# Fetching an expert's second weight matrix in eight gathers of 1 KB rows, and splitting the first in its own order

## The chip, the cores and the metric

The kernel runs on one core of a Trainium2 chip. The metric is device time in microseconds of that core. A core has a matrix engine (TensorE, PE in the profile, its weight loads PEld), VectorE (DVE), ScalarE (ACT), GpSimd (POOL) and SyncE (SP), each with a queue of its own that it works through in order, and 16 DMA engines that all of them feed.

## The reference

The input `x` is 8 sequences of 2496 tokens with 256 features. A Fourier filter along the sequence comes first, then a mixture of 8 experts with a strict capacity.

```python
X = np.fft.rfft(x, axis=1)
y = np.fft.irfft(X * (filt_r + 1j*filt_i)[None], n=x.shape[1], axis=1)   # 8 x 2496 x 256
x = y.reshape(19968, 256)
logits = x @ w_gate                       # 19968 x 8
for idx in np.argsort(-logits.flatten()): # greedy: best pair of token and expert first
    tok, e = idx // 8, idx % 8
    if assigned[tok] < 0 and counts[e] < 2496:
        assigned[tok] = e; counts[e] += 1
for e in range(8):
    h = np.maximum(x[assigned == e] @ w1[e], 0)   # 2496 x 256 by 256 x 1024
    out[assigned == e] = h @ w2[e]                # by 1024 x 256
```

All of it is float32. Every expert ends with exactly 2496 tokens, so its work has a fixed size; which expert is settled next is known only on the chip.

## The kernel before

**Stages.** `Fft` does the filter by matmuls (`s1`, `s2`, `tr`, `inv1`, `inv2`) and writes the filtered tokens to the DRAM buffer `xs` and the logits to `lg`. `Route` finds the assignment in eight phases; each settles one more expert by a search over thresholds (`counts`, `threshold`), and `places` turns it into row numbers: `xid`, where the tokens lie in `xs`, and `oid`, where they belong in `out`. `Ffn` does the experts. From about 526 us on, the product of one expert runs on TensorE while the phases that settle the next ones run in between.

**One expert** (`Ffn.run`) takes its 2496 tokens in five groups of up to 512. `gather` fetches a group's tokens from `xs` in four indirect DMAs of 128 rows of 1 KB each (L814, tile `xg`, 8 buffers). `turn` transposes them on TensorE (L828, tile `ptr`, two halves `h` per group) and splits them into a rounded high part and a low part, by a cast on ScalarE (L831, `xo`) and a subtraction on VectorE (L832, `z`). `first` multiplies by the first matrix, 128 hidden units at a time (f from 0 to 7), in three matmuls for each half of the features (high by high, high by low, low by high; L850, tile `pz`), applies the ReLU and splits the result into `hl` (L856 on ScalarE, L864 or L867 on VectorE, for some of them L860 on GpSimd). Then `run` multiplies by the second matrix (L899, tile `py`, two PSUM buffers), 128 tokens at a time, ScalarE copies the result to `y` (L909, four buffers), and an indirect DMA from GpSimd scatters it to `out` (L910). `pz` and `ptr` share four PSUM buffers. The transposes of the next group stand between the products of the current one: those of group g+1 come after f = 2 and f = 4 of group g.

**The weights.** `Ffn.weights` allocates `raw[0]` and `raw[1]` (tile `wr`, one buffer of 128 x 2048 for each matrix) and the split copies `hl` (two buffers each; the profile shows the first matrix's as `w0h` and `w0l`, the second's as `w1h` and `w1l`). `load(k)` issues an indirect gather from GpSimd (L793) with row numbers `widx` that `expert` computes on VectorE from the expert's number (L659). Each fetches 128 rows of 8 KB. For the first matrix (256 x 1024) partition q gets feature rows 2q and 2q+1. For the second (1024 x 256) partition q gets its rows 8q to 8q+7, so that block f of the products holds the hidden units 8q+f. The columns of the first matrix must then be taken in that order too, and the split of the first matrix reads every eighth column:

```python
src = src.rearrange("p (j q f) -> p j f q", j=2, f=8)[:, j, 4*h:4*h+4]
```

`split` works on a quarter of a matrix at a time: part 0 to 3 are the first matrix's, 4 to 7 the second's. Each is a cast on ScalarE (L807) and a subtraction on VectorE (L808) of 128 x 512.

**What sets the order.** TensorE's order is written out by hand: `Pump` feeds the phases of the routing between the products by lags and due times that stand in the code. The other engines' orders come from a planner that simulates the program with costs of its own and takes what is ready, in the order of the code; `issue_after` pins an instruction behind another on its engine. At the start of the expert stage the code issues the first matrix's gather behind a small copy on GpSimd (L999), then the four splits of the first matrix, the four token gathers of group 0, behind these the gather of the second matrix, the two transposes of group 0, the four splits of the second matrix, and then the run of the expert, whose first act is the token gathers of group 1. For every later expert both matrices are gathered as soon as its phase has found it (`on_w`), while the expert before is still at work, and the splits are dealt out one by one, one for every `PACE` = 5 steps of the products.

Of the kernel before, what the change touches and what calls it, by code (L numbers as in the profile page):

```python
# [8 lines left out]
BF, F16, I32 = mybir.dt.bfloat16, mybir.dt.float16, mybir.dt.int32  # L9
AF, OP, AX = mybir.ActivationFunctionType, mybir.AluOpType, mybir.AxisListType  # L10
# [34 lines left out]
def constants():  # L45
    f = np.float32
    n1, k = np.arange(N1), np.arange(K1)
    c, s = _cs(n1[:, None] * k[None], N1)
# [27 lines left out]
    E = flat(E).astype(f)  # L76
    Eh = _round(E)
    p = np.arange(128)
    row = np.zeros((128, 115))
    row[:, 0:8] = np.arange(8, 0, -1)  # L80
    row[:, 8:16] = np.arange(8)
    row[126, 16] = row[127, 17] = -1
    row[:, 25:32] = G * np.arange(1, 8)
    row[:, 32], row[:, 33], row[:, 34] = p, 64 * (p % 39) + p // 39, p // 39
    pw = np.zeros((128, 11, 7))
    ic = np.zeros((128, 84), np.int64)
# [374 lines left out]
class Route:  # L461
# [10 lines left out]
    def setup(s):  # L472
        nc, i = s.nc, s.i
        t = lambda n, sh, dt=F32: s.cp.tile(sh, dt, name=n)
        s.row = t("row", [128, 115])
        s.pw = t("pw", [128, 11, 7])
        s.ic = t("ic", [128, 84], I32)
        s.tri = t("tri", [117, 118], F16)
# [2 lines left out]
        nc.sync.dma_start(s.ic, i['cInt'])  # L481
        nc.gpsimd.dma_start(s.tri, i['cTri'])
        s.desc, s.eids = s.row[:, 0:8], s.row[:, 8:16]
        s.k22, s.pcol = s.row[:, 25:32], s.row[:, 32:33]
        s.mS = {nj: s.row[:, 40+16*k:56+16*k] for k, nj in enumerate((9, 3, 7))}
        s.mJ = {nj: s.row[:, 88+9*k:88+9*k+nj] for k, nj in enumerate((9, 3, 7))}
        s.ones16 = t("ones16", [128, 128], F16)
# [140 lines left out]
    def phase(s, ph):  # L628

        nc = s.nc  # L630
# [20 lines left out]
        s.want()  # L651
        vc, need, tot, mem = v("vc", [128, 1]), v("need", [128, 1]), v("tot", [117, 4]), v("m0", [117, S])
        tb, pf = v("tb", [117, 2], F16), v("pf", [117, 4])
        ev, ej, eid, widx = v("ev", [128, 8]), v("ej", [128, 8]), v("eid", [128, 1]), v("widx", [128, 1], I32)

        def expert():
            nc.vector.tensor_scalar(ev, s.val, vc, None, op0=OP.is_equal)
            nc.vector.scalar_tensor_tensor(ej, ev, 1.0, s.eids, op0=OP.mult, op1=OP.mult, accum_out=eid)
            nc.vector.scalar_tensor_tensor(widx, eid, 128.0, s.pcol, op0=OP.mult, op1=OP.add)  # L659
        if ph < 7:  # L660
            n = s.n
            T = s.T
# [112 lines left out]
class Ffn:  # L775


    def __init__(s, tc, i, xs, out, cp, ww, zp, ps):
        s.tc, s.nc, s.xs, s.out, s.ww, s.zp, s.ps = tc, tc.nc, xs, out, ww, zp, ps
        s.w1 = i['moe_w1'].rearrange("e (q k) f -> (e q) (k f)", k=2)  # L780
        s.w2 = i['moe_w2'].rearrange("e (q f) d -> (e q) (f d)", f=8)
        s.id = cp.tile([128, 128], F32, name="id")
        make_identity(s.nc, s.id)
        s.scat = []
        s.wt, s.xg, s.xT = {}, {}, {}

    def weights(s, e, widx):
        nc = s.nc
        raw = [s.ww.tile([128, 2048], F32, name=f"wr{k}", bufs=1) for k in range(2)]
        off = bass.IndirectOffsetOnAxis(ap=widx[:, :1], axis=0)  # L790
        hl = [[s.ww.tile([128, 2048], F32R, name=f"w{k}{h}", bufs=2) for h in 'hl'] for k in range(2)]
        s.wt[e] = (raw, hl)
        s.load = lambda k: nc.gpsimd.indirect_dma_start(out=raw[k], out_offset=None, in_=(s.w1, s.w2)[k], in_offset=off).ins  # L793

    def split(s, e, part):

        nc = s.nc
        raw, hl = s.wt[e]
        k, h = divmod(part, 4)
        src, (hi, lo) = raw[k], hl[k]  # L800
        if k == 0:
            h, j = divmod(h, 2)
            src = src.rearrange("p (j q f) -> p j f q", j=2, f=8)[:, j, 4*h:4*h+4]
            hi, lo = (t.rearrange("p (j f q) -> p j f q", j=2, f=8)[:, j, 4*h:4*h+4] for t in (hi, lo))
        else:
            src, hi, lo = (t[:, 512*h:512*h+512] for t in (src, hi, lo))
        nc.scalar.copy(hi, src)  # L807
        nc.vector.tensor_tensor(lo, src, hi.bitcast(F32), op=OP.subtract)  # L808

# [315 lines left out]
```

## Time and profile before

| | |
|---|---|
| runs shown | 1575.35, 1579.18, 1582.28 us (median 1579.18) |
| profiled execution | 1580.15 us, span 1578.4 us |
| granted TensorE clock | 0.958 of full speed, mean |
| TensorE busy | 1419.3 us (90%) |
| VectorE / ScalarE / GpSimd busy | 979.5 / 727.5 / 537.5 us |
| weight gathers (L793) | 16, 16.0 us of GpSimd |
| token gathers (L814) and scatters (L910) | 160 and 160, 171.4 and 173.7 us of GpSimd |
| splits of the first matrix (L808) on VectorE | 32, 36.4 us |
| splits of the second matrix (L808) on VectorE | 32, 21.5 us |

Times in a trace are microseconds from the span's start. A line of a timeline gives the start, the duration, the engine, the source line, the operation, the tile written, the tiles read, the shapes and a count of merged instructions; in brackets stands how long the engine was idle before it and what it then waited for. The waits of an engine are given as total, number and longest. A row of windows gives its length, the busy times of TensorE, its weight loads, VectorE, ScalarE and GpSimd with their numbers of instructions, then the granted clock, the DMA engines' share and GB/s.

### The profile page before, as it was taken

To read this page: it belongs to the slowest core of one execution; us is meant where nothing else is said; L and a number is where in the kernel's file an instruction comes from. 1 tells how busy PE (TensorE), PEld (TensorE's weight loads), DVE (VectorE), ACT (ScalarE), POOL (GpSimd) and SP (SyncE) were. 2 spreads that over 40 slices of the span, in tenths; PEclk is the share of its full clock that TensorE was granted. 3 is DMA by queue.
4 is the path that set the end of the run, shared out by engine and by line. 5 is a ranking of instruction groups with operands and counts; after the bars stand their busy time and mean duration, and the time that the engine had idled before them with its cause. 6 is when DMAs were issued, how large, how long until landed. Compare 5 with 4: busy or idle time off the path is not lost.

```text
span 1578.4 us, 27475 instructions
## 1 busy us (share of the span) xinstructions
PE 1419.3 (90%) x10374; PEld 1240.7 (79%) x10374; DVE 979.5 (62%) x2620; ACT 727.5 (46%) x1703; POOL 537.5 (34%) x557
## 2 busy tenths in 40 slices
PE   2788779799898689999999989999999999999998
PEld 1687658689664378888878878888879889899898
DVE  2677556588544856876776686786696772622322
ACT  4465445566444642643553453453462453632322
POOL 0233223335210242354264434343433443333311
PEclk9899989899979789999999999999999999999999
DMA  8878898845878510211121211211211221111100
GB/s 151 146 111 170 189 186 131 170 93 141 190 217 278 185 53 21 88 59 33 71 63 43 77 45 50 79 51 43 89 44 40 92 98 41 48 44 41 47 28 26
DMA packets 121096, 148.75 MB, mean 94 GB/s; under 512 B 70629, under 2 KB 93755, under 8 KB 118659
## 3 DMA queue, kind: packets, MB, share of 16 engines
q1 hardware_dynamic: 97994, 70.63, 22.6%
q0 software_dynamic: 17840, 60.34, 11.8%
q10 hardware_dynamic: 5129, 16.01, 2.9%
q8 instruction: 82, 1.34, 0.4%
q14 instruction: 51, 0.42, 0.1%
HBM read 84.47 MB, written 62.50 MB: 93 GB/s over the span
## 4 chain that ended last, share of the span: by engine, by line
PE 43%; DVE 10%; issue 7%; ACT 2%; POOL 1%; DMA 1%; another core or an unknown queue 0%; POOLq 0%; DVEq 0%; ACTq 0%
PE py L899 20%; PE pz L850 19%; PE rt L558 2%; PE ptr L828 2%; DVE hl L864 1%; POOL out L910 1%; ACT lg L718 1%; DVE hl L867 1%; DVE w0l L808 1%; DVE w1l L808 1%; DMA wr<-moe_w,widx 1%; DVE Gm L550 1%; DVE OH L749 1%; PE rt L755 1%; DVE tmp L639 0%
## 5 line engine op out<-in xcount | busy, mean ns | idle before, releaser
L899 PE MATMUL py<-w1h,hl 128*128 128x256 f32 x2496 | 485.6, 287 | 3.3 <-DVE hl L867 2.8
L899 PEld LDWEIGHTS py<-w1h,hl 128*128 128x128 f32 x2496 | 403.3, 192 | 7.5 <-DVE hl L867 3.7
L899 PE MATMUL py<-w1l,hl 128*128 128x256 f32 (+1 forms) x1280 | 360.1, 283 | 0.0
L910 POOL DMA_INDIRECT out<-y,oid x160 | 173.7, 1086 | 452.3 <-ACT y L909 410.5
L856 ACT ACTIVATE hl<-pz 128x512 fp32r<-128x512 f32 (+1 forms) x320 | 186.4, 587 | 218.1 <-PE pz L850 182.2
L850 PE MATMUL pz<-xo,w0h 128*128 128x512 f32 (+1 forms) x640 | 265.4, 415 | 12.3 <-DVE hl L864 6.7
L850 PE MATMUL pz<-xo,w0l 128*128 128x512 f32 (+1 forms) x640 | 250.1, 391 | 0.0
L850 PE MATMUL pz<-z,w0h 128*128 128x512 f32 (+1 forms) x640 | 249.3, 389 | 0.8 <-DVE z L832 0.8
L899 PEld LDWEIGHTS py<-w1l,hl 128*128 128x128 f32 (+1 forms) x1280 | 242.3, 189 | 2.0
L864 DVE SCALAR_TENSOR_TENSOR hl<-pz,hl 128x512 fp32r<-128x512 f32 x227 | 155.0, 687 | 121.0 <-ACT hl L856 119.5
L814 POOL DMA_INDIRECT xg<-xs,xid x160 | 171.4, 1071 | 134.3 <-issue 43.3
L909 ACT COPY y<-py 128x256 f32<-128x256 f32 x152 | 56.3, 371 | 294.5 <-PE py L899 254.5
L850 PEld LDWEIGHTS pz<-xo,w0h 128*128 128x128 f32 x640 | 122.7, 192 | 33.6 <-DVE hl L864 9.0
L207 PE MATMUL p<-cS,xr 117*128 117x120 f32 x688 | 102.2, 293 | 42.5 <-ACT xr L195 30.7
L850 PEld LDWEIGHTS pz<-xo,w0l 128*128 128x128 f32 x640 | 121.4, 190 | 24.1
L215 ACT COPY Y<-p 64x240 f32<-64x240 f32 (+1 forms) x304 | 116.0, 381 | 44.0 <-PE p L207 38.3
L850 PEld LDWEIGHTS pz<-z,w0h 128*128 128x128 f32 x640 | 122.3, 191 | 17.3 <-DVE z L832 1.8
L207 PEld LDWEIGHTS p<-cS,xr 117*128 117x128 f32 x688 | 94.0, 208 | 49.0 <-ACT xr L195 30.6
L230 POOL TENSOR_TENSOR P<-P 128x256 f32<-128x256 f32 x80 | 59.7, 746 | 209.6 <-DVE P L228 209.2
L550 DVE TENSOR_TENSOR Gm<-M,thr 117x1232 bf16<-117x1232 f32 (+2 forms) x80 | 104.4, 1316 | 0.2
L222 PE MATMUL p<-cW,Y 128*128 128x128 f32 x640 | 92.9, 280 | 1.3 <-DVE Q L229 1.2
L222 PEld LDWEIGHTS p<-cW,Y 128*128 128x128 f32 x640 | 82.9, 194 | 7.8 <-issue 3.7
(234 smaller groups left out, 2255.8 us busy)
## 6 DMA issues: line engine op xcount, KB each, us to landing
xt<-x SPq DMA_DIRECT2D x24, 838.5 KB
zd<-zt SPq DMA_DIRECT2D x140, 128.0 KB
z<-zd SPq DMA_DIRECT2D x26, 600.0 KB
xs<-xo SPq DMA_DIRECT2D x12, 585.0 KB
xs<-xo ACTq DMA_DIRECT2D x11, 585.0 KB
xs<-Y ACTq DMA_DIRECT2D x9, 585.0 KB
zd<-zt ACTq DMA_DIRECT2D x20, 128.0 KB
xg<-xs,xid POOLq DMA_INDIRECT x160
```

Of the source, the lines that this page charges most:

```text
L207: s.lastmm = nc.tensor.matmul(p[:, q-q0, :120], xv[:, q-24*h], s.cS1, start=True, stop=True).ins
L215: (nc.vector.tensor_copy if t in ((5,) if b else (1, 3, 5, 7, 9)) else nc.scalar.copy)(dst, src)
L222: nc.tensor.matmul(p[:, k], s.Y1[b][:, 4*g+k, dh*128:dh*128+128], s.cW[:, 4*g+k], start=True, stop=True)
L230: nc.gpsimd.tensor_tensor(P[:, :, :64], P[:, :, :64], P[:, :, 64:], op=OP.subtract)
L550: nc.vector.tensor_tensor(Gm[:, s0:s1, :m], s.M[:, s0:s1].unsqueeze(2).to_broadcast([117, s1 - s0, m]), thr[:117].unsqueeze(1).to_broadcas ...
L814: s.lastg = s.nc.gpsimd.indirect_dma_start(out=xg[:n], out_offset=None, in_=s.xs, in_offset=bass.IndirectOffsetOnAxis(ap=ids[0][:n, t:t+1] ...
L850: nc.tensor.matmul(p[:, :n], w[:, sl], x[:, k, :n], start=m == 0, stop=m == 5)
L856: s.lasta = nc.scalar.activation(h[:, :n], p[:, :n], AF.Relu).ins
L864: nc.vector.scalar_tensor_tensor(l[:, :n], p[:, :n], 0.0, h[:, :n].bitcast(F32), op0=OP.max, op1=OP.subtract)
L899: nc.tensor.matmul(p[:a.stop-a.start], hs[g][f][:, a], b[:, 256*f:256*f+256], start=m == 0, stop=m == 8 * len(terms) - 1, skip_group_check ...
L909: s.lasta = nc.scalar.copy(y, p).ins
L910: st = nc.gpsimd.indirect_dma_start(out=out_rows, out_offset=bass.IndirectOffsetOnAxis(ap=ids[1][:w, 4*g+t:4*g+t+1], axis=0), in_=y[:w], i ...
```

## The change

The second matrix is gathered in its own order: eight gathers of 128 rows of 1 KB, gather f fetching rows 128f to 128f+127 into columns 256f to 256f+255 of `raw[1]`. Block f of the products then holds the hidden units 128f to 128f+127, and the split of the first matrix reads 512 neighbouring columns. The order in which its four parts are taken stays: the first halves of both feature rows, then the second halves. `widx` grows from one column to nine, by a second operation on VectorE and eight columns more in the constant `row`.

```diff
-    row = np.zeros((128, 115))
+    row = np.zeros((128, 123))
...
+    row[:, 115:123] = p[:, None] + 128 * np.arange(8)
...
-            nc.vector.scalar_tensor_tensor(widx, eid, 128.0, s.pcol, op0=OP.mult, op1=OP.add)
+            nc.vector.scalar_tensor_tensor(widx[:, 0:1], eid, 128.0, s.pcol, op0=OP.mult, op1=OP.add)
+            nc.vector.scalar_tensor_tensor(widx[:, 1:9], eid.to_broadcast([128, 8]), 1024.0, s.w2rows, op0=OP.mult, op1=OP.add)
...
-        s.w2 = i['moe_w2'].rearrange("e (q f) d -> (e q) (f d)", f=8)
+        s.w2 = i['moe_w2'].rearrange("e f d -> (e f) d")
...
-        off = bass.IndirectOffsetOnAxis(ap=widx[:, :1], axis=0)
...
-        s.load = lambda k: nc.gpsimd.indirect_dma_start(out=raw[k], out_offset=None, in_=(s.w1, s.w2)[k], in_offset=off).ins
+
+        def load(k):
+
+            for f in range(8 if k else 1):
+                o = raw[1][:, 256*f:256*f+256] if k else raw[0]
+                x = nc.gpsimd.indirect_dma_start(out=o, out_offset=None, in_=(s.w1, s.w2)[k],
+                                                 in_offset=bass.IndirectOffsetOnAxis(ap=widx[:, k+f:k+f+1], axis=0))
+            return x.ins
+        s.load = load
...
         if k == 0:
-            h, j = divmod(h, 2)
-            src = src.rearrange("p (j q f) -> p j f q", j=2, f=8)[:, j, 4*h:4*h+4]
-            hi, lo = (t.rearrange("p (j f q) -> p j f q", j=2, f=8)[:, j, 4*h:4*h+4] for t in (hi, lo))
-        else:
-            src, hi, lo = (t[:, 512*h:512*h+512] for t in (src, hi, lo))
+            h = h // 2 + 2 * (h % 2)
+        src, hi, lo = (t[:, 512*h:512*h+512] for t in (src, hi, lo))
         nc.scalar.copy(hi, src)
         nc.vector.tensor_tensor(lo, src, hi.bitcast(F32), op=OP.subtract)
```

More of the change, by code (lines that the diff above doesn't have):

```diff
@@ L474, in setup @@
         t = lambda n, sh, dt=F32: s.cp.tile(sh, dt, name=n)
-        s.row = t("row", [128, 115])
+        s.row = t("row", [128, 123])
         s.pw = t("pw", [128, 11, 7])
@@ L483, in setup @@
         s.desc, s.eids = s.row[:, 0:8], s.row[:, 8:16]
-        s.k22, s.pcol = s.row[:, 25:32], s.row[:, 32:33]
+        s.k22, s.pcol, s.w2rows = s.row[:, 25:32], s.row[:, 32:33], s.row[:, 115:123]
         s.mS = {nj: s.row[:, 40+16*k:56+16*k] for k, nj in enumerate((9, 3, 7))}
@@ L653, in phase @@
         tb, pf = v("tb", [117, 2], F16), v("pf", [117, 4])
-        ev, ej, eid, widx = v("ev", [128, 8]), v("ej", [128, 8]), v("eid", [128, 1]), v("widx", [128, 1], I32)
+        ev, ej, eid, widx = v("ev", [128, 8]), v("ej", [128, 8]), v("eid", [128, 1]), v("widx", [128, 9], I32)
         def expert():
```

## The prediction

> **What bounds the kernel now.** I read the page first, then the waits of TensorE, then the gathers and splits of the weights by tile, then the timelines where they run. The page, engine by engine (busy time, share, instructions):
>
> ```profile
> span 1578.4 us, 27475 instructions
> ...
> PE 1419.3 (90%) x10374; PEld 1240.7 (79%) x10374; DVE 979.5 (62%) x2620; ACT 727.5 (46%) x1703; POOL 537.5 (34%) x557
> ```
>
> TensorE sets the time. The change touches nothing of TensorE's: what it gives or takes must show as TensorE waiting less or more. The waits of TensorE from 526 us to the end (total, times, longest) start with VectorE:
>
> ```profile
> PE rt L755 <- DVE ex L760: 7.4, 5, 3.4
> ...
> PE pz L850 <- DVE hl L864: 6.7, 7, 2.2
> ```
>
> So there is little to win: single waits of 1 to 3 us, each on something that VectorE finishes late.
>
> The change lives in these groups (minimum/median/maximum ns):
>
> ```profile
> L807 ACT CAST w0h<-wr x32: 1120/1200/1250, 533.3 to 1353.9; 128x512 fp32r<-128x512 f32 x32
> L808 DVE TENSOR_TENSOR w0l<-wr,w0h x32: 1070/1152/1207, 534.5 to 1355.4; 128x512 fp32r<-128x512 f32 x32
> L807 ACT CAST w1h<-wr x32: 610/618/649, 540.9 to 1356.5; 128x512 fp32r<-128x512 f32 x32
> L808 DVE TENSOR_TENSOR w1l<-wr,w1h x32: 672/682/710, 543.8 to 1358.4; 128x512 fp32r<-128x512 f32 x32
> L793 POOL DMA_INDIRECT wr<-moe_w,widx x16: 939/966/1385, 526.2 to 1287.1; - x16
> L659 DVE SCALAR_TENSOR_TENSOR widx<-eid,row x8: 145/159/204, 518.5 to 1274.1; 128x1 int32<-128x1 f32 x8
> ```
>
> w0 is the first matrix, read with a step of 8 elements; w1 is the second, read in order. Shapes and types are the same, so the two rows price the step.
>
> **The change part by part.** *The split without a step.* It should cost what w1 costs: 1200 - 618 = 582 ns less on ScalarE, 1152 - 682 = 470 ns less on VectorE, 32 times: 18.6 and 15.0 us of engine time, 2.3 and 1.9 us per expert.
>
> *The gathers.* Two per expert become nine: 56 more in all. One costs GpSimd about a microsecond whatever its bytes, as the rows below show: a gather of tokens (128 rows of 1 KB) and the weight gather (128 rows of 8 KB) take the same. The second index adds one small VectorE operation per expert, at the 159 ns of L659, 1.3 us in all, before a wait for TensorE that is there anyway: I cost it at nothing (bare, +1.3).
>
> What hides the gathers depends on what stands behind them in GpSimd's queue. The first expert is the one without cover. GpSimd there (start, duration, what it waited for):
>
> ```profile
> 534.17 0.95 POOL L814 DMA_INDIRECT xg<-xs,xid  x1 [0.30 <-issue]
> 535.42 0.94 POOL L793 DMA_INDIRECT wr<-moe_w,widx  x1 [0.30 <-PE ptr L828]
> 536.66 1.73 POOL L814 DMA_INDIRECT xg<-xs,xid  x1 [0.30 <-DVE w0l L808]
> ...
> 541.20 0.95 POOL L814 DMA_INDIRECT xg<-xs,xid  x1 [0.30 <-issue]
> 558.77 0.95 POOL L814 DMA_INDIRECT xg<-xs,xid  x1 [16.62 <-PE pz L850]
> ```
>
> The gather at 535.42 is the second matrix; the four from 536.66 to 541.20 fetch the tokens of group 1. ScalarE and VectorE at that place:
>
> ```profile
> 533.33 4.20 ACT L807 CAST w0h<-wr 128x512 fp32r<-128x512 f32 x4 [3.20 <-DMA wr<-moe_w,widx]
> ...
> 538.19 1.07 ACT L831 CAST xo<-ptr 128x512 fp32r<-128x512 f32 x2
> 540.93 2.18 ACT L807 CAST w1h<-wr 128x512 fp32r<-128x512 f32 x4 [1.66 <-DMA wr<-moe_w,widx]
> 543.01 0.59 ACT L856 ACTIVATE hl<-pz 128x512 fp32r<-128x512 f32 x1
> ```
>
> ```profile
> 547.76 1.88 DVE L864 SCALAR_TENSOR_TENSOR hl<-pz,hl 128x512 fp32r<-128x512 f32 x3
> ```
>
> and TensorE, whose order is written out by hand and stays:
>
> ```profile
> 537.00 0.70 PE L828 MATMUL ptr<-id,xg 128*128 128x128 f32 x2 [0.57 <-DMA xg<-xs,xid]
> 539.32 0.79 PE L850 MATMUL pz<-xo,w0h 128*128 128x512 f32 x1 [1.62 <-ACT xo L831]
> ...
> 546.33 0.63 PE L828 MATMUL ptr<-id,xg 128*128 128x128 f32 x4
> 548.50 0.50 PE L850 MATMUL pz<-xo,w0h 128*128 128x512 f32 x1 [1.55 <-DVE hl L864]
> ...
> 551.75 0.67 PE L828 MATMUL ptr<-id,xg 128*128 128x128 f32 x4
> ...
> 557.97 0.28 PE L899 MATMUL py<-w1h,hl 128*128 128x256 f32 x1
> ```
>
> Step 1: the first split is 2.3 us shorter on ScalarE, but the casts xo behind it need the last transposes, which end at 537.00 + 0.70 = 537.70. The second cast can then end near 538.4 and the first matmul start near 538.5 in place of 539.32: 0.8 us early. It runs into the next step and is lost there.
>
> Step 2: eight gathers at the pitch seen (534.17 to 535.42, 1.25 us) hold GpSimd from 535.42 to 545.42. The first token gather of group 1 moves from 536.66 to 545.42, the second to 546.67. A token gather lands 2.83 us after its start (534.17 to the transpose at 537.00): 549.50. TensorE reaches the transpose of 546.33 at about 545.5 and now waits 4.0 us for it. The transposes take 0.63 (0.65 with the hand-over), so the matmul that started at 548.50 starts at 550.15: +1.65 us. Only 1.65 of the 8.76 us of delay shows, since that matmul was waiting for VectorE already. The transposes at 551.75 move to about 553.4, and their tokens (issued 547.92 and 549.17) land by 552.0: no second wait.
>
> Step 3: the second matrix lands in parts, the last at 535.42 + 7 x 1.25 + 2.83 = 547.0 against 540.93. On ScalarE the four casts stand ahead of the first hl, on VectorE the subtractions stand ahead of its hl: 547.0 + 0.62 + 0.68 + 0.69 = 549.0, still ahead of 550.15. If the planner leaves one of the routing's 1.6 us operations in between it is 550.6. The product py at 557.97 has 9 us of cover.
>
> The Trainium skill ("DMA: Bandwidth & Descriptors", Bandwidth) speaks against this edit: batch transfers to at least 1 MiB, since each pays about 2.0 us fixed plus bytes over 436 GB/s. An estimate by that page is 4.4 us for the whole matrix and 2.3 us for each eighth, 18.4 us if they followed each other; by it the matmul of 548.50 would start near 558.6 and the time be near 1588. The trace disagrees with that sum: gathers of this size start 1.25 us apart, so their fixed parts overlap.
>
> Step 4, the seven later experts. The load of expert 1 has its second matrix at 647.14, the next token gather after it, three scatters in between, is
>
> ```profile
> 647.14 1.00 POOL L793 DMA_INDIRECT wr<-moe_w,widx  x1 [0.30 <-issue]
> ...
> 661.46 0.97 POOL L814 DMA_INDIRECT xg<-xs,xid  x1 [2.97 <-PE pz L850]
> ```
>
> Eight gathers end at 657.2, three scatters at 661.1, so the token gather keeps its time. The scatters come up to 6 us late; four y buffers cover that. The tightest other place is expert 6, where two token gathers stand straight behind the load; 8.8 us later they land at 1266.5, and the next transpose is at 1273.93:
>
> ```profile
> 1254.89 0.91 POOL L814 DMA_INDIRECT xg<-xs,xid  x1 [0.30 <-issue]
> ```
>
> ```profile
> 1273.93 0.63 PE L828 MATMUL ptr<-id,xg 128*128 128x128 f32 x4
> ```
>
> At the others the queue holds nothing but scatters until the eight are through. Price: 0, bounds 0 and, if gathers stretch like the 1.73 of 536.66, some 1 us at each of seven.
>
> Step 5, the relief. One wait of TensorE stands straight behind a split on VectorE:
>
> ```profile
> 905.70 1.07 DVE L808 TENSOR_TENSOR w0l<-wr,w0h 128x512 fp32r<-128x512 f32 x1
> 906.69 0.68 DVE L832 TENSOR_TENSOR z<-ptr,xo 128x512 fp32r<-128x512 f32 x1
> ```
>
> ```profile
> 907.42 0.50 PE L850 MATMUL pz<-xo,w0h 128*128 128x512 f32 x1 [1.36 <-DVE z L832]
> ```
>
> It would shrink by 0.47, with the split before it by 0.94. Bounds for all: 0, and 7 x 1.9 = 13.2 us if every nanosecond reached TensorE. Nearest to this row, and with few waits of that kind, I take -2.0.
>
> Sum against the profiled execution's 1580.15 us: +1.65 - 2.0 = 1579.8, so **1580 us**. The median of the runs shown, 1579.18, is 1.0 below that execution, inside their spread of 6.9.
>
> **The rivals.** *The clock falls in the 4 us gap.* Windows of the trace (us, busy times by engine, granted clock, DMA):
>
> ```profile
> 539.00:544.00 5.00, 4.64 (x10) 3.37 (x11) 4.96 (x6) 2.94 (x6) 2.54 (x3) 0.50 0.55 202
> 546.00:549.00 3.00, 1.45 (x9) 1.14 (x8) 3.00 (x5) 1.07 (x2) 0.00 (x0) 1.00 0.00 0
> 566.00:571.00 5.00, 1.65 (x16) 1.03 (x14) 0.00 (x0) 0.18 (x1) 2.92 (x3) 0.77 0.34 103
> ```
>
> The gap of 1.55 us left the clock at 1.00; the thinly used 5 us from 566 took it down. A fresh start ran at 0.50 for about 5.3 us: half of that, 2.6 us, would be lost. Time: 1582.4. The Trainium skill ("TensorE: Matmul & The Clock Gate", Part 1) has one idle window of about 3.4 us bring the slow clock back, the window running freely; by it a 4.0 us gap can fall on either side.
>
> *Gathers go at the pace of their landing* (the other side). If a gather of weights had to land before the next starts, eight would take 8 x 2.83 = 22.6 us; the second token gather of group 1 would start at 560.9 and land at 563.7, the matmul of 548.50 would start at 564.4: +15.9, with the lost clock +18.5: about 1597. It decides from a pitch of 2.1 us on: then the eight take 16.8, the matmul starts at 557.8, and +9.3 less 2.0 is over 0.4%. For it: 1.73 at 536.66. Against: the pitch of 1.25 on the same queue.
>
> *Relief reaches TensorE*: all 13.2 us, 1580.15 + 1.65 - 13.2 = 1568.6. For it: VectorE heads the list of waits. Against: the two rows quoted, 14.1 us together, include many with no split near.
>
> *The planner orders anew.* Only TensorE's order is fixed by hand; changed lengths can shift others. Several waits like the 3.4 and 2.2 us above appear or go: 8 us either way, 1572 to 1588.
>
> *The split is not faster*: if the step is not what w0 pays for, step 1 and 5 vanish: 1581.8. The w1 rows speak against it.
>
> **How the numbers follow.** Forecast 0.42, clock 0.22, new order 0.16, relief 0.11, landing pace 0.07, split not faster 0.02. About 0.5% (8 us) is what a measurement of this kernel can tell from no change. Faster: relief 0.11 and a fifth of the new order, 0.14. Slower: landing pace 0.07 and a third of the new order, with stretched gathers at the seven later loads, 0.13. Same: 0.73. The range 1571 to 1589 leaves out the far ends of relief and landing pace; the likeliest one's own is 1576 to 1585.
>
> **What would show it.** Right: w0 rows near 620 and 680 ns; 72 weight gathers at a pitch near 1.25; TensorE waiting for xg about 4 us near 545 to 550 with its next pz near 550; no xg wait at later loads. Wrong: a pitch above 2 us, scatters so late that ScalarE's y waits for a buffer, a clock of 0.50 after 550, or another order on GpSimd in which the tokens of group 1 go ahead of the eight.

## The result, and the profile after

The changed kernel takes 1622.13 us (median of 4, 1615.71 to 1628.25) against 1580.73 us beside it (1575.35 to 1585.21): a ratio of **1.0251**, 95% interval 1.0223 to 1.0279. It is 41 us slower; the forecast was 1580 us with 1589 as the upper end of its range.

The page's head and the rows of the weights by tile in the profile after (minimum/median/maximum ns):

```profile
span 1619.0 us, 27578 instructions
...
PE 1440.8 (89%) x10374; PEld 1252.1 (77%) x10374; DVE 968.3 (60%) x2628; ACT 712.3 (44%) x1703; POOL 593.7 (37%) x613
```

```profile
L799 POOL DMA_INDIRECT wr<-moe_w,widx x72: 942/949/1847, 520.7 to 1326.8; - x72
L813 ACT CAST w0h<-wr x32: 608/618/633, 527.9 to 1389.7; 128x512 fp32r<-128x512 f32 x32
L814 DVE TENSOR_TENSOR w0l<-wr,w0h x32: 677/683/765, 528.5 to 1390.5; 128x512 fp32r<-128x512 f32 x32
```

The edit did what it says: the first matrix's split costs what the second's did, and there are 72 gathers in place of 16. Lines after the edit have moved: L793 is now L799, L807/L808 L813/L814, L814 L820, L828 L834, L850 L856, L856 L862, L864 L870, L909 L915, L910 L916. GpSimd's 56 us more are the gathers. TensorE is busy 21.5 us longer with the same 10374 matmuls, at a mean granted clock of 0.951 against 0.958.

Where the time went is seen by laying the two traces side by side, by the start of the same matmul in TensorE's fixed order (us; the experts' work begins near matmul 3400):

```
matmul   before    after   after-before   load whose gathers run since the row above (first gather, after)
  3350    512.4    507.0       -5.4
  3650    589.3    586.2       -3.2       expert 0: 520.7
  4100    650.3    648.0       -2.3
  4400    699.4    701.8       +2.4       expert 1: 643.6
  5150    807.6    811.2       +3.6       expert 2: 772.5
  5450    849.2    856.7       +7.5
  5750    890.0    897.7       +7.6
  6050    939.0    954.2      +15.1       expert 3: 903.0
  7400   1130.6   1146.8      +16.1       expert 4: 1026.8
  7700   1176.6   1197.3      +20.7       expert 5: 1150.7
  8300   1259.0   1279.9      +20.9
  8600   1302.7   1339.1      +36.4       experts 6 and 7: 1272.0, 1302.5
 10373   1573.2   1610.0      +36.8
```

The gathers of experts 1 and 6 start 4 and 8 us ahead of the row above. The first row lies ahead of the first weight gather: between the traces of all runs the start of matmul 3350 varies from 507.0 to 516.8 us. From there the first expert, whose delay the forecast worked out, gives 2.2 us by matmul 3650. The next 40 us come in steps, most of them at the seven later loads, priced at nothing; the load of expert 4 gives only 1.0, and 3.9 come between matmuls 5150 and 5450, where no weights are loaded. From matmul 8600 on the curve is flat.

The last 3.8 us lie behind the last matmul. There GpSimd's closing instruction DRAIN, which runs from its last scatter on, takes longer (number, minimum/median/maximum ns; before and after):

```profile
L1121 POOLq DRAIN  x3: 46/97/3164, 1574.4 to 1578.1; - x3
```

```profile
L1127 POOLq DRAIN  x3: 46/97/7018, 1611.2 to 1618.7; - x3
```

Nothing in the forecast has this term; what the instruction waits for no run shows.

One of the steps close up, the load of expert 3. GpSimd's timeline:

```profile
903.03 0.99 POOL L799 DMA_INDIRECT wr<-moe_w,widx  x1 [0.30 <-issue]
...
913.12 0.95 POOL L799 DMA_INDIRECT wr<-moe_w,widx  x1 [0.30 <-issue]
914.38 1.00 POOL L916 DMA_INDIRECT out<-y,oid  x1 [0.30 <-issue]
```

TensorE's:

```profile
908.06 0.28 PE L905 MATMUL py<-w1h,hl 128*128 128x256 f32 x1
...
909.35 0.40 PE L856 MATMUL pz<-xo,w0l 128*128 128x512 f32 x1
...
920.15 1.13 PE L834 MATMUL ptr<-id,xg 128*128 128x128 f32 x4 [7.12 <-DVE hl L870]
```

ScalarE's and VectorE's:

```profile
908.66 0.62 ACT L813 CAST w0h<-wr 128x512 fp32r<-128x512 f32 x1 [2.02 <-DMA wr<-moe_w,widx]
915.29 0.37 ACT L915 COPY y<-py 128x256 f32<-128x256 f32 x1 [6.01 <-remote]
918.77 0.60 ACT L862 ACTIVATE hl<-pz 128x512 fp32r<-128x512 f32 x1 [3.11 <-remote]
```

```profile
919.40 0.69 DVE L870 SCALAR_TENSOR_TENSOR hl<-pz,hl 128x512 fp32r<-128x512 f32 x1 [8.27 <-ACT hl L862]
```

Read them as one story. TensorE's last product py runs at 908.06; ScalarE is free at 909.28 and has only to copy it, but starts at 915.29. The product pz of 909.35 ends at 909.75; ScalarE's ReLU of it starts at 918.77. TensorE had done the work, and ScalarE sat idle and learned of it 7 to 9 us later. Then VectorE was late, then TensorE stood for 7.12 us. In the brackets stands "remote": the view finds no instruction that ended just then. The trace also holds the updates of TensorE's own semaphore: after the one at 905.40 the next is at 915.22, though six of its groups of matmuls ended between, and the other five follow at 918.75 to 918.99 in a heap. GpSimd had begun a run of nine gathers at 903.03 and ended it at 914.07, with a scatter behind it. I call this a **late update**: the instruction has ended, its semaphore moves microseconds later.

Windows of 5 us after the stall (busy times by engine, granted clock, DMA share, GB/s) show what TensorE pays on top:

```profile
920.00:925.00 5.00, 4.12 (x12) 2.81 (x13) 4.03 (x9) 1.79 (x4) 0.00 (x0) 0.50 0.01 3
925.00:930.00 5.00, 5.00 (x24) 4.03 (x24) 3.50 (x10) 4.32 (x13) 0.00 (x0) 0.92 0.00 0
```

After the gap of 7 us the clock is at 0.50 for the next 5 us.

### The profile page after: what moved, and what is told of

Its sections match the earlier page's. It is cut to its first block, busy times and chain, and to the rows that moved or that the text cites. A ratio compares the mean times of both kernels' runs of the same rounds, so it can differ in the third digit from the quotient of the medians.

```text
span 1619.0 us, 27578 instructions
## 1 busy us (share of the span) xinstructions
PE 1440.8 (89%) x10374; PEld 1252.1 (77%) x10374; DVE 968.3 (60%) x2628; ACT 712.3 (44%) x1703; POOL 593.7 (37%) x613
## 4 chain that ended last, share of the span: by engine, by line
PE 44%; DVE 8%; issue 8%; ACT 2%; another core or an unknown queue 2%; POOL 2%; DMA 1%; POOLq 0%; DVEq 0%; ACTq 0%
PE py L905 21%; PE pz L856 19%; PE ptr L834 2%; PE rt L559 2%; DVE hl L870 1%; POOL out L916 1%; DVE hl L873 1%; ACT lg L720 1%; DVE Gm L551 1%; PE rt L757 1%; DMA wr<-moe_w,widx 1%; DVE OH L751 1%; ACT hl L862 0%; DVE w1l L814 0%
## 5 line engine op out<-in xcount | busy, mean ns | idle before, releaser
L905 PE MATMUL py<-w1h,hl 128*128 128x256 f32 x2496 | 491.1, 289 | 7.5 <-issue 5.4
L916 POOL DMA_INDIRECT out<-y,oid x160 | 173.9, 1087 | 418.3 <-ACT y L915 376.0
L862 ACT ACTIVATE hl<-pz 128x512 fp32r<-128x512 f32 (+1 forms) x320 | 186.5, 587 | 247.8 <-PE pz L856 181.8
L856 PE MATMUL pz<-xo,w0h 128*128 128x512 f32 (+1 forms) x640 | 270.2, 422 | 10.4 <-DVE hl L870 4.8
L856 PE MATMUL pz<-z,w0h 128*128 128x512 f32 (+1 forms) x640 | 252.9, 395 | 0.0
L856 PE MATMUL pz<-xo,w0l 128*128 128x512 f32 (+1 forms) x640 | 252.6, 395 | 0.0
L870 DVE SCALAR_TENSOR_TENSOR hl<-pz,hl 128x512 fp32r<-128x512 f32 x227 | 155.2, 687 | 151.9 <-ACT hl L862 141.4
L820 POOL DMA_INDIRECT xg<-xs,xid x160 | 170.1, 1063 | 136.7 <-issue 47.0
L915 ACT COPY y<-py 128x256 f32<-128x256 f32 x152 | 56.5, 372 | 323.3 <-PE py L905 259.2
L856 PEld LDWEIGHTS pz<-xo,w0h 128*128 128x128 f32 x640 | 124.3, 194 | 32.7 <-DVE hl L870 6.7
L856 PEld LDWEIGHTS pz<-xo,w0l 128*128 128x128 f32 x640 | 122.7, 192 | 26.3
L208 PE MATMUL p<-cS,xr 117*128 117x120 f32 x688 | 106.7, 303 | 35.8 <-ACT xr L196 30.8
L856 PEld LDWEIGHTS pz<-z,w0h 128*128 128x128 f32 x640 | 123.9, 194 | 17.1 <-DVE z L838 0.4
L216 ACT COPY Y<-p 64x240 f32<-64x240 f32 (+1 forms) x304 | 116.1, 382 | 42.5 <-PE p L208 36.8
L208 PEld LDWEIGHTS p<-cS,xr 117*128 117x128 f32 x688 | 98.6, 218 | 42.9 <-ACT xr L196 30.8
```

Source lines behind the costliest of these rows:

```text
L208: s.lastmm = nc.tensor.matmul(p[:, q-q0, :120], xv[:, q-24*h], s.cS1, start=True, stop=True).ins
L216: (nc.vector.tensor_copy if t in ((5,) if b else (1, 3, 5, 7, 9)) else nc.scalar.copy)(dst, src)
L820: s.lastg = s.nc.gpsimd.indirect_dma_start(out=xg[:n], out_offset=None, in_=s.xs, in_offset=bass.IndirectOffsetOnAxis(ap=ids[0][:n, t:t+1] ...
L856: nc.tensor.matmul(p[:, :n], w[:, sl], x[:, k, :n], start=m == 0, stop=m == 5)
L862: s.lasta = nc.scalar.activation(h[:, :n], p[:, :n], AF.Relu).ins
L870: nc.vector.scalar_tensor_tensor(l[:, :n], p[:, :n], 0.0, h[:, :n].bitcast(F32), op0=OP.max, op1=OP.subtract)
```

## The experiments

Times are medians in us, ratios to the kernel before on the same chip. One thing has to be known to read them: the runs fell on several chips, and the traces are of two kinds. On three of those that the experiments met, and on the first comparison's, the trace holds late updates; on two others none. I call them **late** and **prompt** chips. Each chip was met at one time only, so whether the kind belongs to the chip or to the hour is not shown. The kernel before takes 1581 to 1587 us on the late ones, 1563 to 1565 on the prompt ones. Counted in the traces after 526 us, for each instruction of TensorE that moves its semaphore: how many had their update recorded more than 2 us after their end (within two, by where the end is put).

```
late chips:    before 17   before again 16   split only 18   plain transfer 14
               changed 40, 41, 37, 39   changed, rows of before 38   gathers only, new rows 43
               gathers spread 32   changed, 16 rows 29
prompt chips:  gathers only 0, 0   four gathers 0, 0   split only 0   eight of 16 rows 0
               step in matmul 0   both plain 0
```

Two things belong to these counts. On the late chips 32 to 42 of TensorE's 1525 updates have no record of their own, in every trace, with the eight gathers or without; on the prompt chips every one has. So some of those counted may be missing records; the waits of ScalarE and VectorE are free of this doubt. And the late ones are not strewn about. GpSimd's scatters are indirect DMAs like its gathers. Where five or more indirect DMAs follow each other with less than 0.7 us between them, the stretch from the first to 4 us behind the last holds all 17 late updates of the profile before and all 40 of the profile after. These stretches are 24% and 33% of the time after 526 us.

**Theory and rivals at the start.** A: an unbroken run of gathers on GpSimd holds the other engines up. B: the shorter split lets the planner order ScalarE and VectorE anew, and that order is worse. C: only the queue at the first expert costs. F: the scatters queue behind the eight gathers, so `y` buffers come late. Further ones came as the results did.

**1. The gathers alone.** (prompt chip)

```diff
 # the changed kernel, with before's split, and
-    row[:, 115:123] = p[:, None] + 128 * np.arange(8)
+    row[:, 115:123] = 8 * p[:, None] + np.arange(8)
```

> Eight gathers of 1 KB rows for the second matrix as in the change, but in the row order of before, with the first matrix split with its step of 8 as before. Theory A (an unbroken run of nine gathers on GpSimd holds up the other engines for 5 to 9 us at each load): about as slow as the changed kernel, 1615 to 1630 us, with the same late spells of TensorE in the loads of experts 1 to 6, because the split has no part in it. Rival B (the shorter split, by which the planner orders ScalarE and VectorE anew, makes the loss): 1578 to 1590 us. Rival C (the gathers cost only their queue at the first expert): 1581 to 1590 us.

1575.58 against 1563.0: 1.0091 (1.0062 to 1.0120). It met none of the three: slower, but by 13 us. At the load that cost 7.12 us above nothing stands still. GpSimd, ScalarE and TensorE in this run:

```profile
888.47 0.99 POOL L799 DMA_INDIRECT wr<-moe_w,widx  x1 [0.30 <-issue]
...
898.94 1.76 POOL L799 DMA_INDIRECT wr<-moe_w,widx  x1 [0.30 <-issue]
901.00 1.00 POOL L919 DMA_INDIRECT out<-y,oid  x1 [0.30 <-issue]
```

```profile
894.24 1.19 ACT L816 CAST w0h<-wr 128x512 fp32r<-128x512 f32 x1 [2.17 <-DMA wr<-moe_w,widx]
895.34 0.36 ACT L918 COPY y<-py 128x256 f32<-128x256 f32 x1
```

```profile
893.50 0.28 PE L908 MATMUL py<-w1h,hl 128*128 128x256 f32 x1
...
900.57 0.50 PE L859 MATMUL pz<-xo,w0h 128*128 128x512 f32 x1 [1.36 <-DVE z L841]
```

The copy of the last product follows the cast without a gap, in the middle of the same run of nine gathers. The scatter behind the run is as late as above. So a run of gathers on GpSimd's queue does not by itself stop the others.

**2. The split alone.** (prompt chip)

```diff
 # the kernel before, with
-            h, j = divmod(h, 2)
-            src = src.rearrange("p (j q f) -> p j f q", ...)
...
+            h = h // 2 + 2 * (h % 2)
```

> The first matrix is split in its own order without a step, the second still comes in one gather of 8 KB rows; the hidden units of the two matrices then do not belong together, so the product is another one, of the same shapes. Theory A: 1566 to 1581 us, no long wait at any load, since the run of gathers is not there. Rival B (the split and the planner's new order): 1605 to 1625 us. The forecast's relief of 2 us would be 1578 us; if all the freed engine time reached TensorE, 1567 us.

1547.70: 0.9903 (0.9873 to 0.9934). B falls: the split is a gain, 15 us, far over the 2 us of the forecast.

**3. Four gathers of 2 KB rows.** (prompt chip; `range(4)`, rows 4p+g, 512 columns each)

> The second matrix in four gathers of 2 KB rows (the row order of before), the first split with its step: the run of gathers at a load is five in place of nine, the bytes are the same. Theory A with a loss that grows with the length of the run: half the loss of eight or less, 1585 to 1603 us, with late spells of 1 to 4 us at a load. Rival D (any split of the gather costs the same, since the wait is on the last landing): 1615 to 1625 us. Rival C: 1580 to 1584 us.

1568.09: 1.0030 (1.0009 to 1.0051), 5 us for 24 gathers more, 0.21 us each; experiment 1 has 12.6 us for 56, 0.22 us each. On this chip a gather has a small price of its own.

**4. The step in the matmul.** (prompt chip)

```diff
-                sl = slice(1024*k+128*f, 1024*k+128*f+128)
+                sl = slice(1024*k+f, 1024*k+1024, 8)
```

> The second matrix in one gather of 8 KB rows as before, the first split in its own order without a step, and the step of 8 moved to the matmul, which loads its 128 columns of the first matrix from every eighth element. Theory A: no run of gathers, so no late spells; if the weight load does not pay for the step, 1566 to 1582 us; if it pays and no longer hides behind the matmul, every one of the 1920 loads of the first product for eight experts grows and the time rises by 20 us or more.

1603.20: 1.0269 (1.0223 to 1.0315). A way around the gathers, and a dear one. The weight loads of the first product, in this run and in the kernel before:

```profile
L847 PEld LDWEIGHTS pz<-xo,w0h 128*128 128x128 f32 x640 | 208.8, 326 | 7.4 <-DVE hl L861 4.4 <-ACT xo L828 1.1 <-PE ptr L825 0.3
```

```profile
L850 PEld LDWEIGHTS pz<-xo,w0h 128*128 128x128 f32 x640 | 122.7, 192 | 33.6 <-DVE hl L864 9.0 <-issue 4.7 <-ACT xo L831 2.0
```

A load with a step of 8 takes 326 ns in place of 192. The matmuls of the first product, 0.23 us apart in the kernel before (545.63 to 545.86 us), stand 0.25 us apart in this run (711.27 to 711.52 us).

**5. The changed kernel again, and whose rows.** The sum of 1 and 2 is about nothing, where the change had cost 2.5%. So the next runs asked whether the rows matter: 128f+p, which lie together, against 8p+f. They fell on a late chip.

> The changed kernel as it is, beside the kernel before on the same chip. If the loss belongs to the kernel: 2 to 3% over the kernel before, with the late spells at the loads of experts 1 to 6 of 5 to 9 us each. If those spells belonged to the executions that were compared first: within 0.5% of the kernel before, since the gathers alone cost 0.9% and the shorter split alone gave 1.0%.

> The changed kernel, in which gather f takes the rows 8p+f of the second matrix in place of 128f+p (only a table of constants differs; every engine has the same instructions in the same order; the hidden units of the two matrices then do not belong together). Theory R (128 rows of 1 KB that lie in one stretch of 128 KB are fetched in a way that holds others up, 128 rows that lie 8 KB apart are not): -1 to +0.5% of the kernel before, no late spells. Theory O (the late spells come of the order in which the planner put the changed kernel's work): 2 to 3% slower, as the changed kernel.

> The first matrix split with its step as before, the second in eight gathers of the changed kernel's rows 128f+p (the same instructions and order as the run of the gathers alone, only the table of constants differs; the hidden units do not belong together). Theory R: slower than the run of the gathers alone, 2 to 3.5% over the kernel before, with late spells of 5 us or more at several loads. Theory O: 0.6 to 1.2% over the kernel before, as the run of the gathers alone.

> The kernel before as it is, for its trace on the chip of these runs: the same time as the kernel before. Of the stall of TensorE at 566 to 571 us behind ten gathers in a row: there again if a run of gathers makes it, gone if it belonged to that one execution.

The kernel before 1586.65 here. Changed again 1634.87, 1.0316 (1.0279 to 1.0353). With the rows of before 1632.87, 1.0297 (1.0264 to 1.0330): **the rows do not matter**, theory R falls. The gathers alone, with the new rows: 1638.93, 1.0347 (1.0304 to 1.0389). O, that the loss hangs on the changed kernel's order, falls with it, since this run has the order of experiment 1. It is experiment 1 in every queue, with another table of constants, on a late chip. Its ScalarE and TensorE at the same load:

```profile
915.70 1.19 ACT L816 CAST w0h<-wr 128x512 fp32r<-128x512 f32 x1 [2.08 <-DMA wr<-moe_w,widx]
924.53 0.37 ACT L918 COPY y<-py 128x256 f32<-128x256 f32 x1 [7.64 <-remote]
```

```profile
915.04 0.28 PE L908 MATMUL py<-w1h,hl 128*128 128x256 f32 x1
...
926.18 1.13 PE L837 MATMUL ptr<-id,xg 128*128 128x128 f32 x4 [6.18 <-DVE hl L873]
```

The same cast, then 7.64 us of nothing before a copy whose product ran at 915.04; the prompt chip has 0. F falls as the main cause: scatters and buffers queue alike in both. The kernel before again is at 1.0001 (0.9973 to 1.0028), and its stall near 566 us, behind eight token gathers with a scatter among them (the expectation counted ten), is there again. Its ScalarE, and that of the first trace of before (waits in 555 to 580 us):

```profile
ACT y L909 <- remote: 9.4, 1, 9.4
```

```profile
ACT y L909 <- remote: 9.2, 1, 9.2
```

**6. Split, spread, plain, on one late chip.** The kernel before 1582.04 here.

> The changed kernel as it is, as the common measure of the four kernels that share this chip. On a chip where semaphore updates come late behind a run of gathers: 2.5 to 3.5% over the kernel before. On a chip where none comes late (as in the traces of the first four experiments): within 0.5% of the kernel before, by the sum of what the gathers alone (+0.9%) and the split alone (-1.0%) gave there.

> The shorter split alone, once more (second matrix in one gather of 8 KB rows; the hidden units do not belong together), beside the changed kernel on the same chip. Theory A: 0.5 to 1.2% faster than the kernel before on every chip, so that the gathers carry the whole loss. Rival B (where updates come late, the new order of the work makes them cost more): 1% slower or more on a chip on which the changed kernel is slower.

1623.52, 1.0266 (1.0217 to 1.0314), and 1571.85, 0.9934 (0.9911 to 0.9956). B falls here too. The two kernels differ by the gathers: 51.7 us for 56, **0.92 us each**, four times the price on the prompt chips. By their traces 45.1 us of it come between matmuls 3650 and 10373, at the later experts, and 3.9 in the closing drain (7.02 us against 3.16).

The gathers in pairs behind scatters:

```diff
+                for _ in range(2):
+                    if s.parts:
+                        with s.tc.issue_after(st.ins):
+                            s.parts.pop(0)()
```

> The changed kernel, with the eight gathers of each of the seven later experts put on GpSimd's queue in pairs, one pair behind each scatter, in place of eight in a row; same instructions, same bytes, the first expert's eight as in the change. Theory A (the length of the unbroken run makes the late spells): the spells of 5 to 9 us at the loads go, the time is within 0.8% of the kernel before, where the changed kernel is 2.5 to 3.5% over it. Rival E (each gather costs its own share, run or no run): 2 to 3.5% over, as the changed kernel. Rival F (the scatters and their buffers behind the eight): part of the loss goes, 1 to 2% over.

1620.16, 1.0250 (1.0205 to 1.0294): no better, and inside rival E's range. ScalarE's waits after 526 us tell why that proves less than it seems. The changed kernel on this chip, and the spread one:

```profile
ACT y L915 <- remote: 28.2, 4, 9.7
...
ACT hl L862 <- remote: 14.9, 6, 4.8
...
ACT xo L837 <- remote: 3.1, 2, 2.2
```

```profile
ACT w1h L820 <- DMA wr<-moe_w,widx: 27.7, 11, 4.9
...
ACT y L922 <- remote: 11.5, 3, 6.8
...
ACT xo L844 <- remote: 2.3, 1, 2.3
...
ACT hl L869 <- remote: 0.6, 1, 0.6
```

ScalarE's waits on late updates fell from 46.2 to 14.4 us, but the pieces now come late, and ScalarE, with a split ahead of its other work, waits 27.7 us for them. VectorE's waits on late updates are about what they were (20.9 us against 23.1), TensorE's late updates are many still (32 against 37), and the longest has grown (10.1 us against 8.3). GpSimd's timeline at the load of expert 1 shows why:

```profile
652.18 0.99 POOL L923 DMA_INDIRECT out<-y,oid  x1 [4.46 <-ACT y L922]
653.47 0.98 POOL L797 DMA_INDIRECT wr<-moe_w,widx  x1 [0.30 <-DVE oa L750]
...
667.60 0.95 POOL L827 DMA_INDIRECT xg<-xs,xid  x1 [0.30 <-issue]
```

Pairs, scatters and token gathers stand in one unbroken run of 13 indirect DMAs, and at the later loads there are runs of up to 20. The edit did not break the run up, so it does not test A: A and E both stay, and the price of a gather that stands alone stays open.

The second matrix by one plain transfer:

```diff
+            r = nc.values_load(widx[0:1, 0:1], engines=[SP], min_val=0, max_val=896, ...)
+            nc.sync.dma_start(raw[1].rearrange("p (f d) -> p f d", f=8),
+                              s.w2[bass.ds(r * 8, 1024)].rearrange("(f p) d -> p f d", p=128))
```

> The changed kernel, with the second matrix fetched by one plain transfer of the whole 1 MiB in rows of 1 KB, issued by SyncE at an address from a register that is loaded from the index table; GpSimd issues no gather of it at all. Same rows, same split, same order of TensorE. Theory A: no run of gathers, so no late spells, and the shorter split is kept: 0.3 to 1.2% faster than the kernel before. Rival G (1024 rows of 1 KB in flight hold the others up, whoever issues them): 1% slower or more.

1587.73, 1.0040 (1.0017 to 1.0063), slower than expected, and 15.9 us over the split alone on this chip. Part of that is lost at the start. Its TensorE and ScalarE there:

```profile
544.24 0.48 PE L757 MATMUL rt<-tab,OH 117*128 117x180 f16 x2 [13.20 <-DVE ex L762]
```

```profile
540.88 2.17 ACT L812 CAST w1h<-wr 128x512 fp32r<-128x512 f32 x4 [10.58 <-DMA wr<-moe_w]
```

The planner put the second matrix's split first on ScalarE, and the transfer issued at 524.30 lets it begin at 540.88. Beside the trace of the split alone, matmul 3350 is 8.4 us later, ahead of the experts' work, matmul 3650 16.1 and the last 16.6: the start costs about 8 us, the seven later loads 0.5. The other part lies behind the last matmul, where the closing drain is three times as long:

```profile
L1126 POOLq DRAIN  x3: 46/103/10530, 1580.0 to 1591.0; - x3
```

It takes 10.53 us against 3.16, 7.4 more; why, no run shows. 14 late updates are what a kernel without the eight gathers has. G falls: at the later loads 1024 rows of 1 KB do no harm when a plain transfer brings them. The Trainium skill ("DMA: Bandwidth & Descriptors", SWDGE vs HWDGE vs iDMA) sends plain transfers to SyncE or ScalarE and keeps GpSimd for the irregular ones. The seven later loads here agree, with 0.5 us against 45.1 for the gathers.

**7. Instruction or rows, and the dose.** (prompt chip; the kernel before 1564.94)

> The run of the gathers alone once more (eight gathers of 128 rows of 1 KB in the row order of before, the first split with its step), as the common measure of the four kernels on this chip. If the chip is one of those where semaphore updates come late: 2.5 to 3.7% over the kernel before, as the same gathers with other rows gave; if it is of the other kind: 0.6 to 1.2% over.

1579.72, 1.0082 (1.0054 to 1.0111): experiment 1 to a tenth of a per cent, on a second prompt chip.

```diff
 # gathers of 16 rows of 8 KB into 16 partitions
-                o = raw[1][:, 256*f:256*f+256] if k else raw[0]
+                o = raw[1][16*f:16*f+16] if k else raw[0]
```

> The same eight gathers for the second matrix at the same places of every queue, but each of 16 rows of 8 KB into 16 partitions in place of 128 rows of 1 KB into all: the same bytes and number of instructions, an eighth of the rows. Theory I (each gather as an instruction costs its share): as slow as the gathers alone beside it, within 0.5%. Theory Q (the rows of a gather cost their share; 1024 more or fewer at a load): within 0.8% of the kernel before where the gathers alone are 2.5% or more over it. Rival F (the work behind the eight on GpSimd's queue): as the gathers alone, since GpSimd is as long at it.

> Four gathers of 128 rows of 2 KB once more: three more instructions than before and 384 more rows at a load, against seven and 896 for eight gathers. Theories I and Q alike: 3/7 of the loss of the gathers alone, so 1.1 to 1.6% over the kernel before if those are 2.5 to 3.7% over. If only an unbroken run beyond some length costs: under 0.6%. If the step from one gather to several costs: over 2%.

Eight of 16 rows: 1572.46, 1.0044 (1.0026 to 1.0062), half the price of eight of 128; 3.1 us of the 7.3 between them are the closing drain, 3.89 us against 7.02. Four: 1566.13, 1.0017 (0.9993 to 1.0041), a fifth of the price for three sevenths of the gathers, though its interval takes in three sevenths of the price too. On a prompt chip the prices are too small to part I from Q.

> Both matrices by plain transfers from SyncE at a register's address, the first matrix ahead of the second, so that at the first expert it does not queue behind the 1 MiB of the second as in the run of the plain transfer; the rows and the shorter split as in the change. Theory: the 11 us lost there at the start go, and the time is 0.4 to 1.2% under the kernel before. If the start still pays for transfers that run beside the fetching of the tokens: 0 to 0.5% over.

1562.40, 0.9985 (0.9963 to 1.0006): no difference that can be told. The start is better than in the other plain run, though TensorE still waits there:

```profile
PE rt L757 <- DVE ex L762: 10.3, 3, 6.4
PE ptr L832 <- DMA xg<-xs,xid: 5.3, 4, 3.6
```

Beside the trace of the split alone (on the other prompt chip) it is 5.3 us later at matmul 3350, 6.4 at matmul 3650 and 8.9 at the last. So the start costs about 1 us, and the larger loss lies at the end again: the closing drain takes 9.96 us against 3.16. Of the 1.0% that the split alone gave, 0.15% is left, and the drain's 6.8 us are the larger half of what went.

**8. The same question on a late chip.** (the kernel before 1580.96)

> The changed kernel as it is. On a chip where updates come late: 2.4 to 3.4% over the kernel before. On a chip where none does: -0.3 to +0.4%, from +0.8 for the gathers alone and -1.0 for the split alone there.

> The changed kernel, with each of its eight gathers fetching 16 rows of 8 KB into 16 partitions (an eighth of the rows, the same bytes; same order of the work on GpSimd and TensorE; the hidden units of the two matrices then do not belong together). On a chip where updates come late: theory Q (the rows cost) within 0.8% of the kernel before; theory I (the instruction costs) 2.4 to 3.4% over it. On a chip where none does: 0.2 to 0.6% below the changed kernel, as with the first split's step (0.44 against 0.82).

The changed kernel 1624.74, 1.0285 (1.0234 to 1.0335). With 16 rows to a gather 1619.50, 1.0239 (1.0197 to 1.0282). An eighth of the rows takes 5 us off 44, 3.1 of them in the closing drain (3.90 us against 7.02), and the intervals overlap: Q falls, **a gather costs as an instruction**, rows are a small part. The Trainium skill ("DMA: Bandwidth & Descriptors", Why a DMA increments its semaphore by 16 and not by 1) says that a DMA from GpSimd has all 16 DMA engines add one to its semaphore whatever its shape. That would fit a price by instruction; that these increments are what delays the others was not tried.

## Why the prediction was wrong

**The step that failed is step 4**, the seven later experts at "Price: 0, bounds 0 and ... some 1 us at each of seven". In the first comparison they cost 40 us net of the shorter split (-3.2 to +36.8 in the table); the gathers' own cost there is 45.1 us, by the changed kernel and the split alone on one late chip. The working of step 4 asked one thing: what stands behind the gathers on GpSimd's queue, and does it come in time? That part held: no token gather came late at a later load. On the prompt chips the 56 gathers cost 13 to 15 us; with 3.9 us of that in the closing drain and about 5 at the first expert, some 4 to 6 us are left for the seven later loads, an estimate, and inside the step's bounds. What the step left out is that with such a run in flight the updates of the other engines can come late, though nothing of theirs stands in that queue. The bound of 1 us was a bound on the queue, not on that.

The signs named for "right" came, the prices of the split, 72 gathers at their pitch, a wait for group 1, no such wait later, and the time was still 41 us off: none of them looked at what ScalarE waited for.

**The row was there.** The windows row of 566 to 571 us, quoted in the prediction, has ScalarE at 0.18 us, VectorE at 0.00 and TensorE at 1.65, behind eight token gathers with a scatter among them, nine indirect DMAs in a row. I used it for what a thin stretch does to the clock and did not ask why it was thin. The timeline of ScalarE in the kernel before answers:

```profile
561.22 0.37 ACT L909 COPY y<-py 128x256 f32<-128x256 f32 x1 [0.18 <-PE py L899]
570.82 0.37 ACT L909 COPY y<-py 128x256 f32<-128x256 f32 x1 [9.23 <-remote]
```

TensorE's product for that copy had ended at 564.06 us; by the trace its update came at 570.80. So 6.7 of the 9.23 us are a late update behind nine indirect DMAs in a row; in the split alone on a prompt chip ScalarE waits 2.51 us at this place (563.65 us). The change makes seven more runs of nine. By that row the price of step 4 is up to 6.7 us at each load, 47 in all, close to the 45.1 measured; a rival worked out from it would have been the right one.

*Step 1* held in its prices: 618 and 683 ns for the first matrix, 620 and 680 forecast. *Step 2* had the right wait and too small a price. GpSimd, and TensorE's wait for group 1:

```profile
530.33 0.95 POOL L799 DMA_INDIRECT wr<-moe_w,widx  x1 [0.30 <-issue]
...
540.00 1.79 POOL L799 DMA_INDIRECT wr<-moe_w,widx  x1 [0.31 <-issue]
542.09 0.95 POOL L820 DMA_INDIRECT xg<-xs,xid  x1 [0.30 <-issue]
```

```profile
533.28 0.80 PE L856 MATMUL pz<-xo,w0h 128*128 128x512 f32 x1 [0.68 <-issue]
...
544.92 0.67 PE L834 MATMUL ptr<-id,xg 128*128 128x128 f32 x2 [5.46 <-DMA xg<-xs,xid]
```

The eight took 11.8 us, 10.0 forecast (two of them stretched to 1.8), and the wait was 5.46 against 4.0. With the start of matmul 3350 as the common zero, the matmul of 548.50 is 3.4 us later than before, 1.65 forecast, and the product py of 557.97 is 5.3 us later. By matmul 3650 only 2.2 us are left, because the stall near 566 us, which both kernels have on a late chip, is shorter after; that this lies near 1.65 is luck. On a prompt chip, where that stall is missing, the way from the first product pz to matmul 3650 takes 48.5 us with the gathers alone and 43.3 with the split alone, 5.2 us more. *The clock rival* (2.6 us) was right in this gap; the 1.9 us between 3.4 and 5.3 are about its price, and the window behind the gap shows its clock:

```profile
545.00:550.00 5.00, 4.43 (x13) 3.08 (x14) 3.14 (x5) 0.74 (x2) 1.68 (x2) 0.50 0.28 79
```

By the Trainium skill ("TensorE: Matmul & The Clock Gate", Part 1) about 3.4 us idle bring the slow clock; 5.46 and 7.12 did. *Step 3*: the splits of the late parts were covered; no wait for them is among TensorE's. *Step 5* had the right sign and the wrong size: -2.0 forecast from two rows; the split alone measured -10.2 us on a late chip (1571.85 against 1582.04) and -15.3 on a prompt one. That is about the rival "relief reaches TensorE" at 13.2, which I held at 0.11. Whether it came through VectorE's 15.0 us or ScalarE's 18.6 was not separated. *The pace of landing* (0.07) was the only rival beyond the range on the slower side; it was a mechanism of the queue and did not come: the pitch stayed near 1.25 us. *A new order* (0.16) does not carry the loss: undoing the split leaves it.

On a late chip the sum is: before, less 10 for the split, plus 52 for 56 gathers. On a prompt chip the parts, +12.6 and -15.3, nearly cancel, so the changed kernel would come out near the kernel before, as forecast; but that would be luck, since the forecast had +1.65 and -2.0 for them. The changed kernel itself was not run there, so this is argued and not shown.

**What stays open**: why some chips show late updates and others none, and whether it is the chip at all; what delays an update; whether a gather that stands alone on GpSimd's queue, with its splits moved back to suit, costs less than 0.92 us, since the spread run left the runs whole; what the closing drain waits for; and whether eight plain transfers would delay updates as eight gathers do, since the plain runs had one at a load, or two.

## What to carry to other kernels

Count indirect DMAs as a possible cost to every engine, not only to the queue that issues them: price one by the worst stretch in the trace where several, gathers or scatters, run together, and ask of each thin window what all the engines in it were waiting for. A wait whose releaser the profile calls remote, with the producer long done, is a sign of it. Look behind the last matmul too: two traces laid side by side by their matmuls leave out what comes after. And before an edit buys engine time with more DMAs, take the two halves apart on the chip: here the one gave 10 to 15 us and the other took up to 52.

## What the runs showed of the hardware that was not expected

- Behind GpSimd's indirect gathers the update of another engine's semaphore can come 7 to 9 us after its instruction's end (908.34 to 915.22 us in the profile after), on three of the five chips of the experiments and in the first comparison; on the two others none of TensorE's was over 2 us late. In the profiles before and after every late one falls in a run of five or more indirect DMAs or at most 4 us behind it.
- The price of one more gather was 0.92 us on a late chip and 0.22 to 0.26 on a prompt one, little changed by its rows: 16 in place of 128 took 5 of 44 us off.
- Loading 128 columns at a step of 8 into TensorE took 326 ns against 192, where the copy with that step took 1200 against 618 on ScalarE.
- GpSimd's closing drain took 3.16 us with 16 weight gathers in the kernel, 4.32 with 40, 7.02 with 72 of 128 rows and 3.9 with 72 of which 64 had 16 rows, on late and prompt chips alike; with one or two plain transfers at each load it took 10.53 and 9.96.
